# Three mask selects per head group, V left unscaled, and a back transform split by parity, in a fused attention and spectral kernel on one core

## Chip, cores and metric

The kernel runs on one core of a Trainium2 chip. The metric is the device time of one execution in microseconds, as the median of several runs. TensorE is called PE (its weight loads PEld), VectorE DVE, ScalarE ACT, GpSimd POOL and SyncE SP, as the profile does.

## What is computed

The input `x` has 2048 tokens of 640 values. Two branches read it, and a gate per token mixes them: `out = g * a + (1 - g) * b`, with `g = sigmoid(sum(x * gate_w))`.

Branch a is attention with a memory, 32 heads of 20 values, in four segments of 512 tokens:

```
for s in range(4):
    p = softmax(q_s k_s^T * scale + causal mask)
    a_dot = p @ v_s
    a_mem = (phi(q_s) @ M) / (phi(q_s) @ z + 1e-6)
    o_s = sigmoid(beta) * a_mem + (1 - sigmoid(beta)) * a_dot
    M += phi(k_s)^T @ v_s ;  z += sum of phi(k_s)
a = concat(o_s) @ wo          # phi(t) = t + 1 where t > 0, else exp(t)
```

Branch b is a filter in the frequency domain: `b = irfft2(rfft2(x) * (w_r + 1j * w_i))` over tokens and values, in float32, then rounded to bfloat16. Softmax is computed without subtracting a maximum, and its sum comes from a column of ones beside V.

## The kernel before

**Order.** The program doesn't rely on program order in Python. `record` (L934) makes a list of some 2300 operations, each with the buffers that it reads and writes and with one or two engines that could run it. The tuple `ORDER` (L708) then lists all of them: an entry halved is the operation's number, and its lowest bit picks the first or second engine of its list. `schedule` (L112) takes each engine's queue from that, gives PSUM banks and DMA semaphores by a small time model, and `emit` (L254) writes the instructions, each engine's in its queue's order, with waits on semaphores. So every engine runs in order, and an instruction that waits holds up all that is behind it on its engine. SP issues nearly all DMAs in the same way. `ENDED` (L586) is a second list, the order in which operations end; it decides only which of several waits of one instruction stands first. Operations made by `either` (L541) may stand on DVE or on POOL, those made by `copy_alts` (L526) on ACT or on DVE, and `one` (L535) names a single engine. `lock` marks DVE operations that the time model lets wait for POOL.

**Attention.** `project` (L1040) makes q, k and V of a segment; q and k go through DRAM (qk_scr) to padded tiles (qkp). `v_part` (L1229) makes V of 128 tokens for half of the heads. For odd blocks of tokens the two halves of 64 tokens change places, which the matmuls do by writing to the two halves of the PSUM bank; one DVE operation (L1244) then evicts 320 columns and multiplies them by 1 - sigmoid(beta) of each head. `attend` (L1294) handles heads in eight groups of four. Two groups make a pair with five units (`UNITS`, `qk_unit`, L1356): kinds a and b for each group and one unit of kind c for both, 80 units in all. A unit's QK matmuls fill four PSUM banks (the whole pool qk), and ACT's exp (L1393) evicts them to the tile ex, which has room for three groups. `PIECES` lists the matmuls; kind a and c use halves of the array 64 columns wide, kind b all 128. After each exp, POOL's selects (`mask`, L1411, at L1414) put zeros above the diagonal, seven per group: two after a, two after b, three after c. Then `pv_flipped` (L1307, segments 0 to 2) or `pv_group` (L1419, segment 3) multiplies by V. `denominators` (L1331) inverts the sums of a segment and sends them through DRAM (r_scr, and r back), after which `normal` (L1656) multiplies them in.

**Spectral branch.** `fft` (L1495) runs beside all this: `fold` (L1020) prepares x, F1 and D are the forward transforms over tokens and values, T twiddles, `W_mul` (L1569) multiplies by the filter, `W_add` (L1574) combines, Tb twiddles back, and Db (L1601) transforms back over values. D uses the parity of the frequency: its evicted result Bt is put in natural order by a write with a stride of two. Db doesn't: each of 16 token residues n2 and each of two types (cosine and sine) takes three matmuls of 321 columns. The cosine bank is evicted to eo in float32 (one of three buffers), and two DVE operations (L1615) add and subtract the sine bank to give the left and the mirrored right half of G.

**End.** `finish_tile` (L1636) makes the last transform over tokens, with the gate in its table (Fb), adds the projection with wo in the same PSUM bank, evicts and stores.

## Time and profile before

| | |
|---|---|
| median of 3 timed runs | 241.27 us (241.19 to 241.69) |
| span of the profiled execution, first to last instruction | 247.9 us |
| mean granted TensorE clock | 0.972 |
| busy: PE, PEld | 230.0, 139.7 us |
| busy: DVE, ACT, POOL | 196.3, 199.7, 165.7 us |
| instructions: DVE, ACT, POOL | 481, 241, 297 |

The profiled execution is one other than the timed ones. Its span is longer than their median by 6.6 us; no time of its own beside the span is given. Busy time is the union of an engine's instructions. A matmul's length holds its passage through the array, so PE counts as busy for longer than columns stream in. Short waits that end in another engine's work are listed by the releaser.

### The profile page before, as it was taken

The numbers are of one execution on the slowest core, as the hardware profiler recorded it, in microseconds if no ns is written. First come the engines' busy times: TensorE is split into PE (matmuls) and PEld (weight loads), VectorE is DVE, ScalarE is ACT, GpSimd is POOL, SyncE is SP. The second block draws the span as 40 slices with busy tenths as digits, with TensorE's granted clock in tenths as the row PEclk, the third lists the DMA queues.
The fourth block names the chain that finished last, engine by engine and source line by source line (L and its number), as shares of the span: only waits on it lengthen the run. The fifth ranks groups of instructions, "written<-read, shape, count | busy, mean of one in ns | idle before, by whom it ended". The sixth has DMA issues, their size and how long they took to land.

```text
span 247.9 us, 9233 instructions
## 1 busy us (share of the span) xinstructions
PE 230.0 (93%) x3849; PEld 139.7 (56%) x3849; DVE 196.3 (79%) x481; ACT 199.7 (81%) x241; POOL 165.7 (67%) x297
## 2 busy tenths in 40 slices
PE   7899999999999999998899999999999975699994
PEld 2574667765465665545566554455444543366794
DVE  0489998799999987888998979979888831755653
ACT  2289688998999989999999899999999864278740
POOL 8532278367969658478939998949898660559640
PEclk9999999999999999999999999999999995599999
DMA  7999979937875864768697543447665977382123
GB/s 174 281 361 206 229 191 230 269 91 203 222 173 163 199 213 114 206 95 252 170 242 208 165 131 99 122 146 192 188 183 128 282 101 81 35 118 81 59 81 109
DMA packets 58924, 42.11 MB, mean 170 GB/s; under 512 B 30020, under 2 KB 55172, under 8 KB 58884
## 3 DMA queue, kind: packets, MB, share of 16 engines
q1 hardware_dynamic: 57844, 40.96, 66.4%
q8 instruction: 30, 0.49, 0.8%
q10 hardware_dynamic: 1040, 0.57, 0.8%
q14 instruction: 10, 0.08, 0.2%
HBM read 23.32 MB, written 12.30 MB: 144 GB/s over the span
## 4 chain that ended last, share of the span: by engine, by line
PE 59%; DVE 15%; DMA 12%; ACT 8%; SPq 3%; issue 2%; DVEq 0%
PE psum L521 52%; PE psum L519 6%; ACT ex L1393 5%; DMA r<-r_scr 3%; DMA r_scr<-rc 3%; DVE Pt L1569 3%; DMA Wt<-in_B_w_i_dram 2%; DMA wk<-in_A_wk_dram 2%; DMA qk_scr<-qu 2%; SPq L553 2%; DVE G L1615 1%; SPq L555 1%; DVE oU L1656 1%; DVE phk L1213 1%; DVE va L1244 1%
## 5 line engine op out<-in xcount | busy, mean ns | idle before, releaser
L1393 ACT ACTIVATE ex<-psum 128x2048 bf16<-128x2048 f32 (+4 forms) x92 | 138.7, 1507 | 13.2 <-PE psum L521 11.4
L1414 POOL TENSOR_SCALAR_AFFINE_SELECT ex<-ex 128x256 bf16<-128x256 bf16 (+2 forms) x224 | 121.0, 562 | 41.2 <-ACT ex L1393 38.3
L521 PE MATMUL psum<-qkp 20*64 20x64 bf16 (+5 forms) x1024 | 31.8, 268 | 4.0 <-ACT ex L1393 2.1
L521 PE MATMUL psum<-xT,wk 128*128 128x256 bf16 (+1 forms) x280 | 33.9, 273 | 0.6 <-DMA wk<-in_A_wk_dram 0.6
L521 PE MATMUL psum<-xT,wq 128*128 128x512 bf16 (+1 forms) x135 | 30.7, 381 | 0.5 <-DMA xT<-in_A_x_dram 0.5
L521 PE MATMUL psum<-wv,xT 128*64 128x320 bf16 (+3 forms) x240 | 30.1, 303 | 0.3 <-DVE va L1244 0.3
L1569 DVE TENSOR_TENSOR Pt<-psum,Wt 128x642 bf16<-128x642 f32 x32 | 25.5, 821 | 2.6 <-PE psum L521 1.5
L521 PEld LDWEIGHTS psum<-qkp 20*64 20x64 bf16 (+1 forms) x1024 | 12.2, 101 | 22.0 <-ACT ex L1393 14.8
L521 PEld LDWEIGHTS psum<-xT,wk 128*128 128x128 bf16 (+1 forms) x280 | 19.9, 97 | 7.1 <-DMA wk<-in_A_wk_dram 1.6
L519 PE MATMUL psum<-wo,oU 128*32 128x320 bf16 x480 | 23.5, 317 | 0.2 <-DVE oU L1664 0.2
L1035 POOL TENSOR_TENSOR xsb<-xf 128x320 bf16<-128x320 bf16 (+2 forms) x12 | 9.5, 788 | 16.2 <-DVE xsb L1035 12.2
L1244 DVE TENSOR_TENSOR va<-psum,ebx 128x320 bf16<-128x320 f32 x32 | 15.2, 483 | 5.0 <-ACT gate L1242 2.9
L521 PEld LDWEIGHTS psum<-wv,xT 128*64 128x64 bf16 (+1 forms) x240 | 14.9, 105 | 7.4 <-issue 2.9
L532 DVE CAST ot<-psum 128x320 bf16<-128x320 f32 x21 | 10.1, 491 | 11.2 <-PE psum L519 8.8
L521 PE MATMUL psum<-big,Cp 128*128 128x321 bf16 (+1 forms) x96 | 18.7, 310 | 0.2 <-DVE G L1615 0.2
L521 PE MATMUL psum<-big,Ac 128*128 128x160 bf16 (+2 forms) x96 | 18.1, 257 | 0.3 <-DVE Pt L1569 0.2
L521 PE MATMUL psum<-ex,va 128*32 128x512 bf16 (+4 forms) x480 | 17.3, 275 | 0.5 <-DVE mem L1289 0.2
L521 PE MATMUL psum<-tt,Yt 128*128 128x256 bf16 (+1 forms) x96 | 16.5, 276 | 1.1 <-DVE Pt L1569 0.4
L1615 DVE TENSOR_TENSOR G<-eo,psum 128x320 bf16<-128x320 f32 x32 | 14.7, 482 | 3.5 <-PE psum L521 2.5
L1201 ACT ACTIVATE et<-qu 128x512 bf16<-128x512 bf16 x25 | 15.6, 629 | 0.2
L519 PEld LDWEIGHTS psum<-wo,oU 128*32 128x32 bf16 x480 | 12.5, 100 | 5.7 <-issue 1.1
L521 PEld LDWEIGHTS psum<-ex,va 128*32 128x32 bf16 x480 | 10.1, 96 | 9.8 <-POOL ex L1414 1.7
(99 smaller groups left out, 393.7 us busy)
## 6 DMA issues: line engine op xcount, KB each, us to landing
qkp<-qk_scr SPq DMA_DIRECT2D x28, 160.0 KB
tt<-tab_tt SPq DMA_DIRECT2D x8, 512.0 KB, 3.8
qk_scr<-qu SPq DMA_DIRECT2D x12, 256.0 KB, 2.4
u_scr<-ub SPq DMA_DIRECT2D x12, 256.0 KB, 4.4
xsb<-in_A_x_dram SPq DMA_DIRECT2D x8, 320.0 KB, 5.9
oU<-u_scr SPq DMA_DIRECT2D x15, 128.0 KB, 4.0
out_dram<-ot SPq DMA_DIRECT2D x12, 160.0 KB
Wt<-in_B_w_r_dram SPq DMA_DIRECT2D x16, 80.2 KB, 3.3
```

The source lines that it names most:

```text
L519: h = e.matmul(dst, wt, r_, start=st, stop=sp_, **{**kw, "tile_position": (0, q), "skip_group_check": True})
L521: h = e.matmul(o_, l_, r_, start=st, stop=sp_, **kw)
L532: alts["dve"] = (lambda e: e.tensor_copy(dst(), src()), 67 + 1.04 * n, 68.0)
L553: return e.dma_start_transpose(d_, s_)
L555: return e.dma_start(d_, s_)
L1035: self.either(lambda e, dst=dst, src=src, d0=d0, n=n, op=op: e.tensor_tensor(xs.ap(o + dst, [D, 2], [1, n]), xf.ap(src + d0, [321, 2], [1, ...
L1201: self.one("act", lambda e: e.activation(et.ap(0, [1, L]), qsl(), ACT.Exp), L, [qb], [b("et", pi_)], late, name="phi_exp")
L1244: self.one("dve", lambda e: e.tensor_tensor(va.ap(i * H * VW + h0 * VW, [VW, nh], [1, DH]), self.ps(bank, 0, [DH, nh], [1, DH]), self.ebx. ...
L1393: self.one("act", lambda e, d=d, q=q: e.activation(self.ex.ap(*d), self.ps(bank, *q), ACT.Exp, scale=SC), n, [bank], [self.exb(s, 2 * pr + ...
L1414: self.one("pool", lambda e: e.affine_select(self.ex.ap(e0 + d0, [1280, 4], [1, n], np_=np_), self.ex.ap(e0 + s0, [1280, 4], [1, n], np_=np_),
L1569: self.one("dve", lambda e, ri=ri, Pt=Pt, Wt=Wt, wo_=wo_, bank=bank: e.tensor_tensor(Pt.ap(ri * 322, [644, 2], [1, KD]), self.ps(bank, 0, ...
L1615: self.one("dve", lambda e, q=q, n2=n2, bank=bank, eo=eo: e.tensor_tensor(self.G.ap(n2 * D + 639 * q, [1 - 2 * q, 320]), eo.ap(q, [1, 320] ...
```

## The change

The change has these parts.

- **Masks.** POOL runs three selects per group in place of seven: `mask_first` (512 elements), `mask_odd` and `mask_even` (1024 each). They follow the third (kind c) unit of the pair for its first group, and the last (second b) unit for its second group. The layout of ex changes for it.
- **QK.** Kind b takes five pieces of 64 columns of the array in place of two of 128, kind c four in place of three. In segment 3 the exps of kind b and c are one operation each, where they were two.
- **V.** V isn't scaled. Odd blocks are projected as the even ones; their eviction is two copies of 64 partitions that change places, on ACT or DVE. The factor 1 - sigmoid(beta) goes into `den_gate` (segments 0 to 2) and into a table g3 (segment 3). A few small operations and one small DMA make these factors.
- **Forward side.** Bt is evicted as it lies, without a stride; W_mul reads W with a stride of two in its place, so that everything up to Db is in order of parity.
- **Back transform.** Db takes matmuls of 322, 161 and 161 columns. The cosine bank goes to eo (two buffers of 644 floats). Two DVE operations put sum and difference with the sine bank into eo, and four operations of 161 or 159 columns (`sum_G`, on DVE or POOL, both inputs in SBUF) make G from these. The table big is 2576 columns wide, not 3220.
- **Order.** `ORDER` is a new list of 2267 operations, and `ENDED` is gone: its place takes the end by the time model. The 80 units stand in the same sequence as before. By the new list sum_G stands 51 times on DVE and 13 times on POOL; V's 48 copies 18 times on ACT and 30 on DVE; folds 44 times on DVE and 4 on POOL (35 and 13 before); the evictions of Db 15 times on ACT and 1 on DVE (10 and 6), those of F1 7 and 13 (11 and 9), those of the first projections 1 and 3 (3 and 1).

```diff
-VPIECES = ((0, 0, 512, 0), (1, 512, 384, 128), (2, 896, 192, 320), (2, 1088, 64, 256), (3, 1216, 128, 384))
+VPIECES = ((0, 0, 512, 0), (1, 512, 128, 128), (1, 896, 256, 256), (2, 640, 256, 256), (3, 1152, 128, 384))
...
-              ((1, 0, 0, 192, 0, 320), (2, 0, 0, 320, 320, 192)),
-              ((2, 0, 0, 256, 0, 64), (3, 64, 64, 384, 0, 128), (3, 0, 0, 448, 64, 64)))
+              ((2, 0, 0, 256, 0, 256), (3, 64, 64, 384, 0, 64), (2, 64, 64, 320, 64, 192), (1, 0, 0, 256, 256, 256), (1, 64, 64, 256, 256, 256)),
+              ((1, 0, 0, 192, 0, 64), (1, 64, 64, 192, 0, 64), (3, 0, 0, 448, 256, 64), (3, 64, 64, 448, 256, 64)))
...
-            for p0, t0, n in ((0, 64, 64), (64, 0, 64)) if i % 2 else ((0, 0, P),):
...
-        self.one("dve", lambda e: e.tensor_tensor(
-            va.ap(i * H * VW + h0 * VW, [VW, nh], [1, DH]), self.ps(bank, 0, [DH, nh], [1, DH]),
-            self.ebx.ap(H + h0, [1, nh], [0, DH]), ALU.mult), nh * DH, [bank, b("omgh")], [vb], prio, name="ev_v")
+        for p0, p1, n in ((0, 64, 64), (64, 0, 64)) if i % 2 else ((0, 0, P),):
+            self.Sc.op(self.copy_alts(lambda p0=p0, n=n: va.ap(i * H * VW + h0 * VW, [VW, nh], [1, DH], p0=p0, np_=n),
+                                      lambda p1=p1, n=n: self.ps(bank, 0, [DH, nh], [1, DH], p0=p1, np_=n), nh * DH),
+                       r=[bank], w=[vb], prio=prio, name="ev_v")
...
+        if u == 3:
+            self.mask(s, 2 * pr, prio)
+        elif u == 4:
+            self.mask(s, 2 * pr + 1, prio)
...
+        x = [self.exb(s, g, k) for k in ("a0", "b0", "c0", "m0")]
+        self.one("pool", sel(512, 0, 64, 64, P), 512, x[:2], x[3:], prio, per=0.793, fix=218, name="mask_first")
+        self.one("pool", sel(512, 512, P, -64, 64), 1024, [], x[2:], prio, per=0.793, fix=218, name="mask_odd")
+        self.one("pool", sel(0, 0, P, 0, P), 1024, [], x[:2], prio, per=0.793, fix=218, name="mask_even")
...
-                for c in range(3):
+                for n_, (c, c0, n, tc) in enumerate(((1, 0, 322, 161), (0, 0, 161, 0), (2, 161, 161, 483))):
...
+                for q, op in enumerate((ALU.add, ALU.subtract)):
+                    self.one("dve", lambda e, q=q, op=op, bank=bank, eo=eo: e.tensor_tensor(
+                        eo.ap(322 - 322 * q, [1, 322]), eo.ap(0, [1, 322]), self.ps(bank, 0, [1, 322]), op),
+                        322, [bank, eb[0]][:2 - q], [eb[1 - q]], prio, name="sum_Db", after=[b("xT", i, c) for i in range(k + 1) for c in range(5)] if not q else ())
+                o = n2 * D
+                for d0, d1, step, n, t, op in ((0, 0, 1, 161, 322, ALU.add), (1, 319, -1, 159, 0, ALU.subtract), (0, 320, 1, 161, 322, ALU.subtract),
+                                               (1, 639, -1, 159, 0, ALU.add)):
+                    fn = lambda e, d0=d0, d1=d1, step=step, n=n, t=t, op=op, o=o, eo=eo: e.tensor_tensor(
+                        self.G.ap(o + d1, [step, n]), eo.ap(t + 161 + d0, [1, n]), eo.ap(t + d0, [1, n]), op)
+                    self.Sc.op({"dve": (fn, 67 + 1.04 * n, 68.0), "pool": (fn, 132 + 1.95 * n, 50.0)}, r=[eb[t > 0]], w=[b("G", n2, d1 // 320 if d1 != 320 else 1)],
+                               prio=prio, name="sum_G", after=acb, lock=True)
```

186 lines of the change are left out of this document (84 added, 102 removed), and 310 rows, old and new, of tables (ENDED, ORDER).

## Prediction

> **What bounds the kernel now.** I read the busy table by stretch of time first, cut where the exponential (ex, L1393) of attention unit 0, 8, 16, 56, 64 and 72 starts (of 80, counted from 0), because both orders run the 80 units in the same sequence. Columns: stretch, its length, then busy us of PE, PEld, DVE, ACT and POOL with their instruction counts, granted clock, DMA share, GB/s.
>
> ```profile
> core 0 of [0], span 247.9 us
> core 0: us, PE busy (x) PEld busy (x) DVE busy (x) ACT busy (x) POOL busy (x), PEclk, DMA share, GB/s
> 13.50:49.00 35.50, 35.16 (x438) 23.93 (x437) 32.35 (x79) 31.25 (x49) 17.79 (x31) 1.00 0.99 244
> 49.00:71.10 22.10, 21.41 (x301) 12.28 (x298) 21.20 (x58) 20.21 (x24) 15.59 (x30) 1.00 0.70 183
> 71.10:168.00 96.90, 93.30 (x1366) 53.67 (x1364) 86.68 (x206) 91.59 (x102) 74.42 (x139) 1.00 0.62 166
> 168.00:186.50 18.50, 17.48 (x275) 9.45 (x278) 16.77 (x50) 17.34 (x21) 16.72 (x30) 1.00 0.67 190
> 186.50:215.10 28.60, 22.03 (x503) 12.83 (x499) 17.78 (x45) 17.63 (x21) 15.33 (x27) 0.80 0.67 125
> 215.10:247.90 32.80, 29.59 (x828) 22.00 (x824) 17.09 (x40) 18.58 (x23) 17.02 (x31) 0.97 0.43 89
> ```
>
> The reader is to see three full engines. Up to 186.5 us PE, ACT and DVE are each busy 88 to 99% of every stretch; from 71 to 168 ACT leaves 5.3 us of 96.9 free and DVE 10.2. POOL, which the change relieves most, has the least to do in each. After 186.5 us DVE and ACT have room, and PE has the work.
>
> The chain of waits shows the one long hole, in the stretch from 186.5 (columns: start, us, what):
>
> ```profile
> 195.92 6.75 DMA r_scr<-rc
> 202.69 7.07 DMA r<-r_scr
> 209.78 1.77 DVE oU L1656 x5
> ```
>
> The third segment's reciprocal denominators go to DRAM and back in 13.8 us, and DVE, PE and ACT stand in line behind the five products that need them: PE is busy for 22.03 of 28.60 us, 6.6 us idle, at a clock of 0.80. The profiled execution spans 247.9 us, the median of the timed runs is 241.27, 6.6 us less; so part of this hole may not be there in the timed runs. I sum against the 247.9 and carry the difference over to 241.27.
>
> **The change part by part.** Engine and place of every operation were counted in the two orders, which name them by number.
>
> *Back transform (Db).* Before, three matmuls of 321 columns for each of 32 banks; after, one of 322 and two of 161. The forward transform has this shape already (columns: min/median/max ns; 321 is its longest form, 160 and 161 the short ones):
>
> ```profile
> L521 PE MATMUL psum<-big,Ac x96: 230/240/310, 49.6 to 153.8; 128*128 128x160 bf16 x32, 128*128 128x321 bf16 x32, 128*128 128x161 bf16 x32
> L521 PE MATMUL psum<-big,Cp x96: 297/301/475, 166.5 to 206.5; 128*128 128x321 bf16 x64, 65*128 65x321 bf16 x32
> ```
>
> 301 against about 236 for a short one (between the 230 and the 240) is 65 ns, twice per bank: 32 x 0.13 = 4.2 us less on PE, between 166 and 207 us. There ACT and DVE are as full as PE, and after 186.5 PE's idle time is the hole. I credit 1.0; the bounds are 0 and 4.2.
>
> *QK.* The second kind of unit goes from 8 matmuls 128 columns wide to 20 that are 64 wide; the first kind has that width now, in 12:
>
> ```profile
> 123.08 0.40 PE L521 MATMUL psum<-qkp 20*128 20x320 bf16 x8 [0.23 <-ACT ex L1393]
> ...
> 125.67 0.43 PE L521 MATMUL psum<-qkp 20*64 20x512 bf16 x12
> ```
>
> The same 512 columns stream past both halves of the array together, so 0.03 us more, x32 = 1.0 us; were each change of weights in the three-piece half to cost that again, 3 us. All four qk banks are one buffer, so exp waits for QK: I take +1.0 on the path (0 to 3).
>
> *V and its eviction.* DVE's 32 scaled evictions become 48 plain copies, 18 on ACT and 30 on DVE. In segment 3 the second exp is no longer split in two, nor the third. Db's evictions move by 5 from DVE to ACT, F1's by 4 and the first projections' by 2 the other way.
>
> ```profile
> L1393 ACT ACTIVATE ex<-psum 128x2048 bf16<-128x2048 f32 x56 | 105.2, 1879 | 7.9 <-PE psum L521 6.7
> ...
> L1393 ACT ACTIVATE ex<-psum 128x1024 bf16<-128x1024 f32 x12 | 12.3, 1023 | 1.1 <-PE psum L521 0.8
> ...
> L1393 ACT ACTIVATE ex<-psum 128x1280 bf16<-128x1280 f32 x8 | 9.9, 1239 | 3.0 <-PE psum L521 3.0
> L530 ACT ACTIVATE Ac<-psum 128x512 bf16<-128x512 f32 x11 | 6.5, 603 | 1.2 <-PE psum L521 1.2
> L1393 ACT ACTIVATE ex<-psum 128x768 bf16<-128x768 f32 x8 | 6.5, 810 | 0.3
> L530 ACT ACTIVATE Bt<-psum 128x322 bf16<-128x322 f32 x12 | 6.3, 541 | 1.5 <-PE psum L521 1.4
> ...
> L1393 ACT ACTIVATE ex<-psum 128x512 bf16<-128x512 f32 x8 | 4.8, 598 | 1.1 <-PE psum L521 1.0
> L530 ACT ACTIVATE ot<-psum 128x320 bf16<-128x320 f32 x11 | 4.7, 436 | 10.7 <-PE psum L519 8.1 <-PE psum L521 1.7 <-DMA out_dram<-ot 0.8
> L530 ACT ACTIVATE eo<-psum 128x321 f32<-128x321 f32 x10 | 4.1, 438 | 0.3 <-PE psum L521 0.3
> ```
>
> ACT: +18 x 0.436 + 5 x 0.438 = +10.0; -8 x (1.239 + 0.810 - 1.879) - 4 x (2 x 0.598 - 1.023) = -2.1; -6 x 0.603 = -3.6; Bt is written without a stride, -12 x 0.10 (541 against 438 ns) = -1.2; eight fewer one-column gate exps on top, unpriced. Net +3.1 at most. By the orders the excess lies before 49 us, where ACT has 4.3 us free; behind that its load is level. +0.5 (0 to 3.1).
>
> *DVE, early.* Nine fold operations come over from POOL, and six F1 and projection evictions from ACT:
>
> ```profile
> L1035 DVE TENSOR_TENSOR xsb<-xf x20: 310/324/844, 9.0 to 34.9; 128x320 bf16<-128x320 bf16 x8, 128x318 bf16<-128x318 bf16 x6, 128x322 bf16<-128x322 bf16 x6
> ```
>
> 9 x 0.32 = 2.9 us, and 6 at no less than ACT's 0.60 = 3.6; three V copies and four other projection evictions come after 49 us instead, 7 x 0.48 (G's 320 columns from PSUM, below) = 3.4. Net about +3 by 71 us, where DVE is busy for 53.6 of 57.6 us. What waits behind these in DVE's queue is V's eviction and phi of k, and PE behind their banks. I take +2.0 (0 to 3).
>
> *DVE, late.* Before, G came from PSUM in two operations per n2. After, two go to a float buffer, and four of about 160 columns, with both inputs in SBUF, make G: 64 in all, 51 on DVE (22 of them between 168 and 186.5 us, 22 between 186.5 and 215, 7 later), 13 on POOL.
>
> ```profile
> L1120 DVE TENSOR_TENSOR ebg<-gate,ebx x1: 257/257/257, 54.7 to 54.7; 128x128 f32<-128x128 f32 x1
> ```
> ```profile
> 186.34 1.67 DVE L1615 TENSOR_TENSOR G<-eo,psum 128x320 bf16<-128x320 f32 x4
> ```
> ```profile
> L1615 DVE TENSOR_TENSOR G<-eo,psum x32: 475/481/489, 169.2 to 217.5; 128x320 bf16<-128x320 f32 x32
> ```
> ```profile
> L1574 DVE TENSOR_TENSOR Yt<-Pt x16: 314/320/719, 56.0 to 161.7; 128x321 bf16<-128x321 bf16 x16
> ```
>
> From 257 ns at 128 columns and 481 at 320 (1.17 ns a column) 160 columns take 0.29 us. Four G operations in 1.67 us start every 0.40, 0.08 under their length, so each new one takes 0.21 of DVE's time: 51 x 0.21 = 10.7 us. And they wait: an operation with one PSUM input never strays (475 to 489), one with two SBUF inputs has the same median as minimum and a longest of 719 beside 314, with POOL running. At 0 to 0.4 us each that is 0 to 20 us; I take 0.1, 5 us. From 168 to 186.5, 22 x 0.31 = 6.8 us come to a DVE with 1.7 free; against that stand 4 fewer of the old G operations and 3 Db evictions (7 x 0.40 = 2.8), and by the counts 0.5 of smaller ones. 6.8 - 3.3 - 1.7 = 1.8; I take +1.5 (0 to 8.4, the end worked out with the rival). From 186.5 on DVE has 26 us free, and I charge nothing.
>
> By the Trainium skill, "SBUF — State Buffer", "Who interferes with whom", a DVE instruction with two SBUF inputs contends with a GpSimd instruction that reads SBUF, and whichever issues first holds the shared pair for its whole length. The spread of Yt beside that of G agrees. By this rule alone a G operation could wait out a whole select, which is the rival on DVE below.
>
> *Masks.* POOL runs seven selects per head group now, three after (one of 512, two of 1024 elements):
>
> ```profile
> L1414 POOL TENSOR_SCALAR_AFFINE_SELECT ex<-ex 128x256 bf16<-128x256 bf16 x128 | 59.5, 476 | 38.7 <-ACT ex L1393 37.4
> L1414 POOL TENSOR_SCALAR_AFFINE_SELECT ex<-ex 64x512 bf16<-64x512 bf16 x64 | 42.6, 670 | 1.8 <-ACT ex L1393 0.9
> L1414 POOL TENSOR_SCALAR_AFFINE_SELECT ex<-ex 128x512 bf16<-128x512 bf16 x32 | 22.0, 690 | 0.6
> ```
>
> Per group 4 x 0.476 + 2 x 0.670 + 0.690 = 3.9 us before; 0.84 ns an element (690 less 476 over 256) gives 0.69 + 2 x 1.12 = 2.9 after: 32 us of POOL in all. POOL waited 37.4 us for exp, so this is off the path. But three selects can run only when the group's last exp is there. At the end:
>
> ```profile
> 231.07 5.36 POOL L1414 TENSOR_SCALAR_AFFINE_SELECT ex<-ex 128x256 bf16<-128x256 bf16 x10 [1.71 <-ACT ex L1393]
> ```
> ```profile
> 233.69 2.08 ACT L1393 ACTIVATE ex<-psum 128x1280 bf16<-128x1280 f32 x2 [0.91 <-PE psum L521]
> ```
>
> The last exp ends at 235.77, the last mask at 236.43, 0.66 us later; after, 2.9. The same delay stands before the second-last unit's exp, whose buffer is freed by those products. PE has some 2 us of projections placed in between. +1.0 (0 to 4).
>
> *The hole.* In the new order the first product that needs the third segment's denominators stands two QK units later, behind 1.02 + 1.88 = 2.9 us of exp, and the read-back follows the write at once on SP. If the 13.8 us trip recurs that is -2.9; if the timed runs have no hole, 0. I take -1.0. In exchange for Bt, DVE's 32 products with W read W with a stride of two. No row shows that: 0 to the 0.10 us of ACT's strided write for each half, 6.4 us in all; I take 0, as they read PSUM at its own pace beside it. Two float buffers in place of three cost nothing as long as DVE keeps up; what if not stands in the slow rival.
>
> Sum: -1.0 + 1.0 + 0.5 + 2.0 + 1.5 + 1.0 - 1.0 = +4.0 us: 251.9 in a profiled execution like this one, **245.3** as a median.
>
> **The rivals.**
>
> *Faster: PE's relief counts in full.* PE is the fullest engine of the first table. Every us of Db's 4.2 then shortens the end, DVE's additions fit into its free time (26 us after 186.5), and the hole gains its 2.9; QK's +1.0 and the tail's +1.0 stay: -5.1, 236.2. It decides by whether DVE keeps 95% or less between 168 and 200 us. For it: DVE's share there before is 91% and lower. Against it: ACT and DVE are at their limit when Db begins. Chance 0.30.
>
> *Slower by much: DVE becomes the bound.* Each two-input G operation waits 0.4 us, and ACT, whose Db evictions need the float buffers that DVE frees, stalls with it: 22 x 0.61 = 13.4 us, less the 1.7 free and the 3.3, is +8.4; with the early 2.0 and the tail's 1.0, +11.4: 252.7. The skill's exclusive lock is this mechanism; its price here is from the longest Yt. Chance 0.17.
>
> *Nothing moves:* ACT's exps pace the kernel, the early excess fits into the 4.3 us of ACT and 3.2 of DVE, and the tail is hidden: 241 to 241.7. Chance 0.05.
>
> *The selects don't cost what I say* (runs of 64 elements might be dearer than the slope): a third dearer, and POOL is as full as before (32 x 3.9 us), the tail 1 us longer: 246.3. This lies inside the forecast.
>
> **How the numbers follow.** Forecast, +0.6 to +8 us around its +4.0 (down 3.4 where Db and the hole each count 2.7, up 4.0 where the early DVE term and the tail reach their 3 and 4): 0.48. With the rivals: faster by over 0.2% 0.30, within 0.2% 0.05 (0.2%, half a us, is about what a measurement of this kernel can tell from no change), slower 0.65. The range runs from the fast rival to the slow one, 236.0 to 253.0, and leaves out 2 in 10. The forecast's own range is 242 to 249.
>
> **What would show it.** Busy time of DVE up by 12 to 18 us, of POOL down by 25 to 35, of PE down by 2 to 5, ACT within 3: these say that the pieces are priced rightly. The stretch from unit 56 to unit 64 longer than 18.5 us with DVE over 95% says that late DVE work sets the pace; G operations spread from 0.29 to 0.7 us say that they wait for selects. If that stretch is no longer, and the end from unit 64 shorter than 61.4 us, the fast rival is right. Last mask 2 to 3 us behind the last exp: the tail. The prediction is wrong if POOL's relief moves the exps themselves, that is, if unit 56 comes earlier than 168 us: then waits for masks paced the middle, which the first table doesn't show.

## The result, and the profile after

The changed kernel takes **254.54 us** (median of 4 runs, 253.54 to 255.66), the kernel before 241.23 in the same comparison (4 runs): a ratio of 1.0536, 95% interval 1.0496 to 1.0575. The forecast was 245.3. The direction was right, the size three times too small: +13.3 us against +4.0, and outside the range.

The profile after, cut at the same exponentials (units 0, 8, 16, 56, 64 and 72 of 80, counted from 0), columns as in the prediction:

```profile
13.30:49.80 36.50, 35.88 (x453) 23.75 (x452) 34.60 (x91) 34.62 (x57) 9.69 (x12) 1.00 0.89 215
49.80:72.90 23.10, 21.97 (x347) 12.80 (x346) 22.84 (x58) 20.86 (x27) 13.69 (x20) 1.00 0.70 172
72.90:170.90 98.00, 92.52 (x1606) 55.81 (x1605) 91.98 (x223) 90.32 (x99) 63.00 (x82) 1.00 0.68 169
170.90:194.00 23.10, 17.74 (x321) 8.80 (x320) 21.94 (x60) 17.52 (x20) 13.68 (x18) 0.71 0.68 187
194.00:217.20 23.20, 20.43 (x537) 13.06 (x532) 22.55 (x62) 18.04 (x19) 12.00 (x13) 0.99 0.58 123
217.20:253.60 36.40, 31.14 (x887) 22.62 (x886) 23.91 (x59) 18.21 (x19) 14.00 (x16) 0.94 0.35 85
```

In the prediction's profile the stretch from unit 64 to 72 took 28.6 us, because of the 13.8 us trip of the reciprocals through DRAM. A second profile of the old queues (run b_ctl below: its own time is 242.44 us, its span 240.4) shows what the timed runs of the kernel before look like:

```profile
13.60:49.20 35.60, 35.26 (x438) 23.95 (x437) 32.28 (x79) 31.24 (x49) 17.76 (x31) 1.00 1.00 241
49.20:71.30 22.10, 21.41 (x300) 12.24 (x298) 21.23 (x58) 20.23 (x24) 15.63 (x30) 1.00 0.74 182
71.30:167.80 96.50, 93.22 (x1367) 53.86 (x1365) 86.82 (x206) 91.40 (x101) 74.27 (x139) 1.00 0.64 168
167.80:186.30 18.50, 17.47 (x275) 9.45 (x278) 16.76 (x50) 17.34 (x21) 16.71 (x30) 1.00 0.68 189
186.30:207.50 21.20, 20.09 (x507) 12.26 (x503) 17.31 (x44) 17.52 (x21) 14.77 (x27) 1.00 0.82 166
207.50:240.40 32.90, 28.88 (x828) 21.51 (x820) 17.55 (x41) 18.50 (x23) 17.81 (x31) 1.00 0.49 91
```

Read one table against the other: +0.9 and +1.0 us up to unit 16, +1.5 to unit 56, **+4.6 from unit 56 to 64** (+4.4 with unrounded starts, as below), +2.0 to unit 72, **+3.5 behind it**; 13.5 together, against 13.3 timed. In the two stretches from 56 to 72 DVE is busy for 44.5 of 46.3 us, where it was busy for 34.1 of 39.7. PE goes from 94% busy in the first of them to 77%. The busy times of the whole execution, of the second profile of before and of after:

```profile
PE 227.8 (95%) x3849; PEld 138.8 (58%) x3849; DVE 196.4 (82%) x481; ACT 199.4 (83%) x241; POOL 165.8 (69%) x297
```
```profile
PE 230.8 (91%) x4281; PEld 141.7 (56%) x4281; DVE 219.4 (87%) x551; ACT 201.5 (79%) x238; POOL 131.2 (52%) x168
```

POOL gave up 34.6 us and DVE took on 23.0. What the pieces of G cost on each engine (min/median/max ns), and their groups with the selects (busy us, mean ns, idle time before them):

```profile
L1491 DVE TENSOR_TENSOR G<-eo x51: 314/321/1294, 173.5 to 230.6; 128x161 bf16<-128x161 f32 x26, 128x159 bf16<-128x159 f32 x25
L1491 POOL TENSOR_TENSOR G<-eo x13: 519/538/697, 172.5 to 222.8; 128x159 bf16<-128x159 f32 x7, 128x161 bf16<-128x161 f32 x6
```
```profile
L1283 POOL TENSOR_SCALAR_AFFINE_SELECT ex<-ex 64x1024 bf16<-64x1024 bf16 (+2 forms) x96 | 92.5, 979 | 35.3 <-ACT ex L1271 31.3
L1491 DVE TENSOR_TENSOR G<-eo 128x161 bf16<-128x161 f32 (+1 forms) x51 | 20.7, 448 | 0.0
```

A piece that waits for nobody takes 0.32 us, the longest 1.29, which is 0.32 and one whole select (0.979) more. The trace shows what the long ones wait for. 32 of the 51 overlap no operation of POOL, and none of them takes more than 0.33 us. The eleven over 0.5 us all started while an operation of POOL ran (eight times a select, three times a piece of G there), and each ended 0.18 to 0.24 us after that one's end. The chain of waits runs through them at that point (start, us, what):

```profile
173.55 2.62 DVE G L1491 x7
176.17 0.60 DVE fbg L1043
...
182.05 0.24 DVE G L1491
182.29 0.67 DVE oU L1533 x2
182.96 1.91 DVE G L1491 x2
```

Of the seven pieces in 2.62 us one took 1.24 us behind a select, and the five behind it start every 0.23 us; the two in 1.91 us (0.78 and 1.29) both waited for selects.

### The profile page after: what moved, and what is told of

Its sections match the earlier page's. It is cut to its first block, busy times and chain, and to the rows that moved or that the text cites. A ratio compares the mean times of both kernels' runs of the same rounds, so it can differ in the third digit from the quotient of the medians.

```text
span 253.6 us, 10064 instructions
## 1 busy us (share of the span) xinstructions
PE 230.8 (91%) x4281; PEld 141.7 (56%) x4281; DVE 219.4 (87%) x551; ACT 201.5 (79%) x238; POOL 131.2 (52%) x168
## 4 chain that ended last, share of the span: by engine, by line
PE 54%; DVE 29%; ACT 9%; issue 4%; DMA 2%; SPq 0%; DVEq 0%
PE psum L525 49%; ACT ex L1271 8%; PE psum L523 5%; DVE G L1491 5%; DVE eo L1485 4%; DMA xT<-in_A_x_dram 2%; DVE xsb L923 2%; DVE Pt L1438 1%; DVE ub L536 1%; DVE Cp L536 1%; DVE va L536 1%; DVE oU L1533 1%; DVE phq L1105 1%; DVE xf L918 1%; DVE ot L536 1%
## 5 line engine op out<-in xcount | busy, mean ns | idle before, releaser
L1271 ACT ACTIVATE ex<-psum 128x2048 bf16<-128x2048 f32 (+1 forms) x80 | 136.5, 1706 | 16.2 <-PE psum L525 13.8
L1283 POOL TENSOR_SCALAR_AFFINE_SELECT ex<-ex 64x1024 bf16<-64x1024 bf16 (+2 forms) x96 | 92.5, 979 | 35.3 <-ACT ex L1271 31.3
L525 PE MATMUL psum<-qkp 20*64 20x64 bf16 (+4 forms) x1536 | 33.7, 259 | 4.5 <-ACT ex L1271 4.0
L525 PE MATMUL psum<-wv,xT 128*128 128x321 bf16 (+1 forms) x160 | 29.3, 300 | 0.0
L525 PEld LDWEIGHTS psum<-qkp 20*64 20x64 bf16 x1536 | 14.9, 105 | 23.6 <-ACT ex L1271 16.9
L1438 DVE TENSOR_TENSOR Pt<-psum,Wt 128x644 bf16<-128x644 f32 x32 | 26.0, 820 | 1.6 <-PE psum L525 1.2
L1491 DVE TENSOR_TENSOR G<-eo 128x161 bf16<-128x161 f32 (+1 forms) x51 | 20.7, 448 | 0.0
L525 PE MATMUL psum<-big,Cp 128*128 128x322 bf16 (+2 forms) x96 | 16.1, 284 | 3.4 <-DVE mem L1177 1.2
L525 PE MATMUL psum<-ex,va 128*32 128x256 bf16 (+2 forms) x480 | 18.4, 286 | 0.6 <-POOL ex L1283 0.6
L1443 POOL TENSOR_TENSOR Yt<-Pt 128x322 bf16<-128x322 bf16 x18 | 13.3, 749 | 9.8 <-DVE Pt L1438 7.7
L525 PE MATMUL psum<-big,Ac 128*128 128x161 bf16 (+2 forms) x96 | 16.2, 257 | 0.1
L1093 ACT ACTIVATE et<-qu 128x512 bf16<-128x512 bf16 x25 | 15.5, 625 | 0.5 <-DVE phq L1106 0.5
```

What stands on the lines that cost most here:

```text
L525: h = e.matmul(o_, l_, r_, start=st, stop=sp_, **kw)
L1093: self.one("act", lambda e: e.activation(et.ap(0, [1, L]), qsl(), ACT.Exp), L, [qb], [b("et", pi_)], late, name="phi_exp")
L1271: self.one("act", lambda e: e.activation(self.ex.ap(*d), self.ps(bank, *q), ACT.Exp, scale=SC), n, [bank], [self.exb(s, 2 * pr + gp, ks) f ...
L1283: return lambda e: e.affine_select(self.ex.ap(e0 + d0, [640, 8], [1, n], np_=np_), self.ex.ap(e0 + s0, [640, 8], [1, n], np_=np_), [[0, 8] ...
L1438: self.one("dve", lambda e, ri=ri, Pt=Pt, Wt=Wt, wo_=wo_, bank=bank: e.tensor_tensor(Pt.ap(ri * 322, [644, 2], [161, 2], [1, 161]), self.p ...
L1443: fn = lambda e, r=r, a0=a0, a1=a1, op=op, Pt=Pt, Yt=Yt: e.tensor_tensor(Yt.ap(r * 322, [1, 322]), Pt.ap(a0 * 322, [1, 322]), Pt.ap(a1 * 3 ...
```

## The experiments

Three theories stood at the start, a fourth came on the way. T1: the pieces of G on DVE, and the port that they share with POOL's selects. T2: late masks. T3: the new order by itself. T4: PE's clock. Kernels whose name begins with a_ are made from the changed kernel, those with b_ from the one before. Where a part of one kernel was put into the other, all remaining operations kept their queues, and new ones were put where their inputs end by the planned times. The table gives the ratio to the kernel before (95% interval) and, from the trace of each, the us between the starts of exponentials 0, 16, 56, 64, 79 and the end.

| run | ratio | 0–16 | 16–56 | 56–64 | 64–79 | 79–end |
|---|---|---|---|---|---|---|
| b_ctl | 1.003 (0.998–1.008) | 57.7 | 96.5 | 18.6 | 39.8 | 14.3 |
| after | 1.0536 (1.050–1.058) | 59.6 | 98.0 | 23.0 | 42.0 | 17.7 |
| a_noS | 1.038 (1.031–1.045) | 59.6 | 98.0 | 18.8 | 43.1 | 17.3 |
| a_Gsmall | 1.030 (1.020–1.040) | 59.6 | 98.0 | 20.2 | 39.8 | 17.6 |
| a_selsmall | 1.019 (1.010–1.028) | 57.9 | 97.2 | 21.0 | 38.4 | 17.1 |
| a_noS_sel | 1.025 (1.018–1.033) | 58.0 | 97.8 | 18.8 | 41.4 | 17.6 |
| a_sellock | 1.039 (1.032–1.046) | 58.4 | 98.4 | 20.4 | 42.5 | 17.4 |
| a_sellock2 | 1.040 (1.031–1.050) | 57.9 | 98.2 | 22.0 | 41.3 | 17.8 |
| a_fill | 1.049 (1.042–1.056) | 60.0 | 98.7 | 23.1 | 41.4 | 16.9 |
| a_eo3 | 1.050 (1.041–1.059) | 60.1 | 98.5 | 23.3 | 41.4 | 17.3 |
| a_tail | 1.061 (1.049–1.072) | 60.4 | 98.0 | 23.0 | 43.6 | 18.7 |
| a_Gpool | 1.074 (1.067–1.081) | 59.7 | 98.2 | 25.4 | 45.8 | 17.3 |
| a_noV | 1.075 (1.070–1.081) | 61.3 | 103.1 | 23.4 | 42.0 | 16.2 |
| a_noM | 1.133 (1.123–1.142) | 64.0 | 102.4 | 27.7 | 47.5 | 17.2 |
| b_F | 0.997 (0.994–1.000) | 58.0 | 95.7 | 18.6 | 38.1 | 14.3 |
| b_selsmall | 0.995 (0.991–0.999) | 58.4 | 95.3 | 18.6 | 39.1 | 14.2 |
| b_V | 1.047 (1.038–1.055) | 62.5 | 100.2 | 18.8 | 41.3 | 15.2 |
| b_S3 | 1.084 (1.079–1.088) | 58.4 | 95.7 | 31.9 | 46.9 | 14.2 |
| b_M | 1.131 (1.122–1.140) | 64.1 | 106.9 | 22.8 | 48.0 | 18.2 |

### The split out of the changed kernel, and its pieces cut short

a_noS takes the forward side and the back transform of before into the changed kernel (the 64 entries of sum_G leave the order). a_Gsmall is:

```diff
-                        self.G.ap(o + d1, [step, n]), eo.ap(t + 161 + d0, [1, n]), eo.ap(t + d0, [1, n]), op)
+                        self.G.ap(o + d1, [step, 8]), eo.ap(t + 161 + d0, [1, 8]), eo.ap(t + d0, [1, 8]), op)
...
-                            self.G.ap((4 * a + q) * D + 320 * hf, [1, 320]), True, False,
+                            self.G.ap((4 * a + q) * D + 320 * hf, [0, 40], [1, 8]), True, False,
```

> The changed kernel with its three selects and unscaled V, but with the forward side and the back transform of before (Bt written with a stride, Db in three matmuls of 321 columns, G made from PSUM in two operations per n2, three float buffers of 322), in the new order without the 64 sum_G operations. Theory T1 (the pieces of G on DVE are the loss: 51 x 0.448 us, and what stands behind them): DVE's busy time falls by some 20 us from 219, the stretch from the 57th to the 72nd exponential is 6 us or more shorter, and the time is 242 to 246 us. Theory T2 (late masks: three selects of 0.98 us that can start only after the last exponential of their group): the time stays at 251 to 255 us. Theory T3 (the new order by itself, whatever the operations): 250 to 255 us, with DVE less busy and PE idle instead.

> The changed kernel with each of the 64 sum_G operations cut to 8 of its 161 or 159 columns; the rest of G isn't made, and the last transform reads the same 8 columns over and over, in as many matmuls of the same size. All waits and the order stay. T1: DVE loses 51 x some 0.3 us = 15 us or more, the time falls by 7 to 11 us to 244 to 248 us. T2: the time stays within 2 us of 254.5. T3: it stays within 3 us.

Both miss T1's time: the medians are 252.8 and 250.6 us, or 250.4 and 248.4 by the ratios. DVE's busy time fell by 15.5 and 11.5 us, less than T1 said, and in a_noS the stretch from the 57th to the 72nd exponential got only 2.5 us shorter, not 6; by its median alone a_noS fits T2 and T3. T1's place is right for the first part of that stretch. Units 56 to 64, cut out of the trace of a_noS, with the next row (64 to 72):

```profile
170.80:189.60 18.80, 15.01 (x321) 7.81 (x321) 14.45 (x38) 17.18 (x19) 7.63 (x9) 1.00 0.64 179
189.60:215.70 26.10, 24.04 (x541) 14.37 (x536) 18.54 (x42) 17.97 (x20) 11.26 (x12) 0.87 0.75 146
```

18.8 us, against 23.0 with the split and 18.6 before: in this stretch the split is the whole loss, and DVE's load is its form (14.45 us in place of 21.94). But a part of the gain is given back at once: the next row takes 26.1 us, 2.9 more than in the changed kernel. There the chain has two DMAs, one behind the other in SP's queue:

```profile
189.57 6.29 DMA u_scr<-ub
...
197.88 5.16 DMA gbc<-g_scr
```

So the whole split, with its stalls, is worth 1.5% here, and the columns of the pieces alone 2.4% (the two intervals overlap). With the short pieces the units 64 to 79 take 39.8 us, as in b_ctl. Pieces of 8 columns still take 0.15 us each, and the longest waits nearly as long (0.92 us over the shortest, where it was 0.98):

```profile
L1491 DVE TENSOR_TENSOR G<-eo x51: 148/158/1065, 173.0 to 225.3; 128x8 bf16<-128x8 f32 x51
```

### The split alone in the old order

The forward side and the split, with three float buffers, in the kernel before; sum_G stands behind its second sum.

> The kernel before with the forward side and the split back transform of the change alone, with three float buffers, the sum_G operations right behind their second sum (51 on DVE and 13 on POOL as in the change); seven selects, scaled V and the other queues as before. T1: DVE's busy time rises by some 18 to 25 us from 196, and the time by 4 to 8 us to 245 to 250. If the split is worth something to PE, it rises by 2 or less.

+8.4%, some 20 us, beyond every theory. The row of units 56 to 64 and the pieces of G:

```profile
166.90:197.90 31.00, 22.14 (x264) 11.64 (x265) 29.05 (x76) 17.95 (x21) 21.56 (x38) 0.61 0.45 125
```
```profile
L1509 DVE TENSOR_TENSOR G<-eo x51: 266/501/1914, 169.0 to 227.5; 128x161 bf16<-128x161 f32 x26, 128x159 bf16<-128x159 f32 x25
```

Up to unit 56 and in the tail it is as fast as b_ctl (58.4, 95.7, 14.2 us); all of the loss lies where Db is. The median piece takes 0.50 us here, 0.32 in the changed kernel, as 29 of the 51 take more than 0.4 us and not 11. The number of selects alone doesn't do this: a_noM (below), with seven per group in the new order, has a median of 0.32 and 19 such pieces. How often a piece meets a select depends on the order, too.

### The selects cut short

In a_selsmall two of the three selects handle 64 elements in place of 1024; b_selsmall cuts the five that work in place in the kernel before to as many (`[1, 16]` in four runs).

```diff
-            return lambda e: e.affine_select(self.ex.ap(e0 + d0, [640, 8], [1, n], np_=np_), self.ex.ap(e0 + s0, [640, 8], [1, n], np_=np_),
-                                             [[0, 8], [1, n]], ALU.is_ge, 0.0, base=base, channel_multiplier=-1)
+            return lambda e: e.affine_select(self.ex.ap(e0 + d0, [640, 8], [1, 64 if d0 != s0 else 8], np_=np_), self.ex.ap(e0 + s0, [640, 8], [1, 64 if d0 != s0 else 8], np_=np_),
+                                             [[0, 8], [1, 64 if d0 != s0 else 8]], ALU.is_ge, 0.0, base=base, channel_multiplier=-1)
```

The expectation of b_selsmall names two ratios: they are those of a_noS and a_selsmall.

> The changed kernel with two of its three selects (1024 elements) cut to 64 elements; so most of the upper triangle is not set to zero. POOL loses some 55 us or more of busy time. T1 with the lock: G operations fall from a mean of 0.448 to 0.33 us with a maximum below 0.7, folds and Yt become shorter too, the gain of 3 to 6 us arises between the 57th and the 72nd exponential, and the tail (from the last exponential to the end) gives at most 2 us. T2: the tail shortens by 2 us or more and the middle units come earlier; G operations keep their length. Both give a time of 248 to 252 us; the place of the gain and the length of the G operations tell them apart.

> The kernel before with five of its seven selects per group (those in place) cut to 64 elements, so that most of the upper triangle is not set to zero: the control for the same cut in the changed kernel, which gave 1.0381 - 1.019 and more. If POOL's selects slow DVE's two-input operations by the lock in any kernel, DVE's busy time falls by 3 to 8 us here too (196 before) and the time by 1 to 4 us. If the price is that of late masks, which this kernel doesn't have, the time stays within 1 us.

The largest gain of all in the changed kernel, 1.0536 to 1.019 (8.4 us by the ratios), and 0.5% in the kernel before, where DVE's busy time falls by 3.1 us (196.4 to 193.3). In a_selsmall DVE's falls by 9.2, and half of that is G:

```profile
L1491 DVE TENSOR_TENSOR G<-eo x51: 306/319/799, 170.7 to 221.7; 128x161 bf16<-128x161 f32 x26, 128x159 bf16<-128x159 f32 x25
```

The same medians, but a longest of 0.80, where T1 said less than 0.7. The tail hardly shortens (17.1), which speaks against T2 at that place; the gain lies in 0–16, 56–64 and 64–79. The cut takes away load and lateness at once. These two put the load back, on memory that nobody else reads:

```diff
...
+        for _ in range(3):
+            self.one("pool", lambda e: e.affine_select(self.idle.ap(0, [1, 352]), self.idle.ap(0, [1, 352]), [[1, 352]], ...), 352, [], [self.b("idle")], ...)
```

> The changed kernel with two of its three selects cut to 64 elements, as in a_selsmall, and behind the last of each group three selects of 352 elements on memory of their own that no other instruction reads (32 x 3 x some 0.5 us = 48 us of POOL, about what the cut took away, 52). Nothing on the path waits for them but the next group's selects. If POOL's load on the shared port was the price, G operations go back from a mean of 0.358 to 0.42 us or more, DVE's busy time from 210 to 215 or more, and the time from 247.8 to 251 to 255 us. If the lateness of the masks was the price, the time stays at 246 to 250 us.

> As a_sellock (two of three selects cut to 64 elements; 96 selects of 352 elements on memory that no other instruction reads, 47 us of POOL), but the added selects stand in POOL's queue only where it had a gap of at least their length before its next mask. If POOL's load on the shared port is the price, the time is 250.5 to 254 us again and DVE's busy time 214 us or more. If lateness is the price, the time is 247 to 249 us, DVE's busy time may still be 214.

Both came to 252 us: of the 8.4, some 5 come back with the load. DVE's busy time is 215.0 and 214.7 (210.2 without), a piece of G takes 0.40 us on average (0.36 without, 0.45 in the changed kernel). In a_sellock2 the masks don't get late again. What follows the last exponential there, which ends at 235.13 us:

```profile
235.19 1.25 POOL L1290 TENSOR_SCALAR_AFFINE_SELECT ex<-ex 128x512 bf16<-128x512 bf16 x3 [1.87 <-ACT ex L1278]
237.29 0.79 POOL L1339 TENSOR_TENSOR on<-on,mem 128x320 bf16<-128x320 bf16 x1 [0.84 <-DVE on L1334]
238.03 1.66 POOL L1297 TENSOR_SCALAR_AFFINE_SELECT idle<-idle 128x352 bf16<-128x352 bf16 x3
```

The last mask ends 1.3 us behind that exponential, as in a_selsmall (2.9 in the changed kernel). Measured in every group against the same exponential (the one after which its first mask can run), the last mask ends 5.2 us later on average, 5.1 in a_selsmall and 6.4 in the changed kernel. So POOL's load by itself is the larger part of the 8.4 us. The remaining 3 go with late masks or with the load that isn't back (POOL is busy for 124.7 us, not 131.2); these two aren't told apart. By place the load counts in 64–79 (38.4 us without it, 42.5 and 41.3 with it). In 0–16 it doesn't: 57.9 us in a_sellock2 with POOL busy there for 22.4 us (23.4 in the changed kernel).

### All pieces on POOL, and three float buffers

a_Gpool sets the lowest bit of all 64 entries of sum_G in the order. a_eo3 is:

```diff
...
-        self.eo = [T(f"eo{i}", [P, 644], F32, at=self.xT[0].off + i * 2592) for i in range(2)]
+        self.eo = [T(f"eo{i}", [P, 644], F32, at=self.xT[0].off + i * 2592) for i in range(3)]
...
-                k = n2 % 2
+                k = n2 % 3
...
```

> The changed kernel with all 64 sum_G operations on POOL, none on DVE; otherwise the same order. T1: DVE's busy time falls by 18 us or more, POOL's rises by 51 x 0.54 = 28 us; selects and G operations stand in one queue, so the masks come later; the time falls by 2 to 6 us if DVE's load was the price. T2 (late masks): it rises by 2 us or more.

> The changed kernel with three float buffers eo of 644 columns in place of two (the broadcast reciprocals of the third segment move to other memory). If ACT's evictions of Db, which waited 3.9 us for DVE's G operations, stall the exponentials and PE, the time falls by 1.5 to 4 us. If DVE's own queue is what counts, the time stays within 1 us of 254.5.

On POOL a piece takes 0.53 us (median of 64), and the ratio is 1.074, 4.9 us slower than the change, as T2 had it. T1's own number missed: DVE lost the 20.7 us of its pieces, and its busy time fell by 2.5 us only (219.4 to 216.9). Other operations with two inputs in SBUF took the time, as they now wait for POOL's pieces. Two of them, first in the changed kernel, then in a_Gpool:

```profile
L1043 DVE TENSOR_TENSOR fbg<-fcat,gbc x4: 670/682/814, 176.1 to 233.5; 128x512 bf16<-128x512 bf16 x4
L1541 DVE TENSOR_TENSOR oU<-oU,mT x8: 481/484/1449, 201.3 to 236.7; 128x640 bf16<-128x640 bf16 x8
```
```profile
L1043 DVE TENSOR_TENSOR fbg<-fcat,gbc x4: 679/844/5157, 171.6 to 238.0; 128x512 bf16<-128x512 bf16 x4
L1541 DVE TENSOR_TENSOR oU<-oU,mT x8: 481/756/4643, 199.8 to 241.0; 128x640 bf16<-128x640 bf16 x8
```

The operation of 5.16 us met a select on POOL, seven pieces and one more select ran there one behind the other, and it ended 0.55 us after the last of them: it didn't get in between. So moving work to POOL didn't free DVE. Three buffers gain nothing that can be seen (1.050, the intervals lie on one another): the stall of ACT behind the two float buffers, a part of the slow rival, had no price that these runs resolve.

### PE's clock

In the changed kernel the clock is halved for the time in which the most is lost. Four stretches of its trace; the seventh number is the granted clock:

```profile
173.80:177.20 3.40, 2.17 (x62) 1.23 (x54) 3.40 (x9) 2.65 (x4) 1.02 (x1) 1.00 0.92 128
177.20:180.60 3.40, 1.88 (x43) 1.00 (x44) 3.37 (x10) 3.15 (x4) 1.80 (x4) 1.00 0.85 279
180.60:194.30 13.70, 11.59 (x168) 5.25 (x168) 12.28 (x35) 9.17 (x10) 8.33 (x10) 0.50 0.59 179
194.30:197.70 3.40, 2.68 (x51) 1.45 (x49) 3.23 (x8) 3.00 (x3) 1.16 (x2) 1.00 0.41 118
```

Is this cause or consequence? a_fill gives PE more to do just there:

```diff
-                    self.mms([(th, n)], cpb + [b("big"), bank], [], prio, name="Db", mode=0)
+                    self.mms([(th, n)] * (3 if n_ == 0 and 1 <= n2 <= 5 else 1), cpb + [b("big"), bank], [], prio, name="Db", mode=0, ...)
```

> The changed kernel with more to do for PE and nothing else: in the ten banks of Db of n2 = 1 to 5, which stand between 170 and 188 us, the first matmul (322 columns) is issued three times, each overwriting the one before; the result is the same. A third theory, T4 (PE's clock): in the profiled run of the changed kernel PE was busy for only 56% of the 3.4 us before 180.64 us, and from there on the granted clock was 0.50 for 13.65 us. T4: with 2.7 us more of matmuls in this place PE stays above some two thirds, the clock stays at 1.00, PE's busy time falls from 230.8 to some 228 in spite of the added work, the stretch from the 61st to the 65th exponential takes 10 to 11 us in place of 13.3, and the time falls by 3 to 6 us to 249 to 252. T1 (DVE alone sets the pace there, 97% busy): the clock may rise, but the time stays within 1.5 us of 254.5, or rises.

```profile
173.80:177.20 3.40, 2.81 (x69) 1.69 (x62) 3.36 (x11) 2.54 (x5) 0.68 (x2) 1.00 0.98 114
177.20:182.50 5.30, 3.92 (x88) 2.14 (x80) 5.23 (x16) 4.99 (x7) 3.03 (x4) 1.00 0.75 212
182.50:185.90 3.40, 1.41 (x41) 0.88 (x41) 3.40 (x10) 2.27 (x3) 2.34 (x3) 1.00 0.32 90
185.90:192.80 6.90, 6.44 (x76) 2.56 (x76) 6.15 (x19) 3.62 (x4) 3.48 (x6) 0.51 0.80 251
```

The clock stayed whole for 7 us longer (180.6 and 185.9 us; the first exponential was at 13.3 and 11.2), the halved stretch shrank from 13.7 to 6.9 us, and units 56 to 64 took 23.1 us, no less than without (23.0). DVE is the busy column in the first three rows (3.36 of 3.40, 5.23 of 5.30, 3.40 of 3.40). T4 falls, as a price of 3 to 6 us: DVE sets the pace, PE starves, and the halved clock follows.

### The tail

The last QK, the work behind it and the last store, cut at the last exponential's start and at PE's end: b_ctl, after, and a_tail, which moves twelve of PE's operations ahead of the last QK.

```profile
226.10:237.20 11.10, 11.02 (x316) 9.73 (x315) 6.64 (x17) 4.50 (x7) 4.30 (x8) 1.00 0.26 78
237.20:240.40 3.20, 0.00 (x0) 0.00 (x0) 0.47 (x1) 0.00 (x0) 0.00 (x0) 1.00 0.45 127
```
```profile
235.90:249.00 13.10, 13.05 (x384) 11.27 (x379) 8.19 (x22) 5.03 (x7) 4.24 (x5) 1.00 0.27 83
249.00:253.60 4.60, 0.00 (x0) 0.00 (x0) 0.49 (x1) 0.00 (x0) 0.00 (x0) 0.86 0.30 83
```

PE is never idle up to its end; it has 384 matmuls behind the last exponential's start, not 316, and takes 2.0 us longer. From PE's end to the end it is 4.6 us in place of 3.2. This goes with one part of the change: in the 13 profiles of kernels with unscaled V, whose SP issues 233 DMAs and not 232, it is 3.8 to 4.8 us, in the 7 with scaled V 3.2 to 3.3. The traces place the difference: near PE's end one issue of a store on SP, on ACT or on both takes 0.9 to 2.2 us in the former, and in the latter none takes more than 1.0, some 2.5 us earlier. Why is open. Of the 68 more matmuls 40 are products of the exponentials with V, which now come behind later masks, and 28 belong to Fb and to products with wo. The products with V in the same stretch, of b_ctl and of after:

```profile
L519 PE MATMUL psum<-va,ex 128*128 128x21 bf16 x80 | 2.5, 172 | 0.0
```
```profile
L525 PE MATMUL psum<-va,ex 128*128 128x21 bf16 x120 | 3.3, 172 | 0.0
```

> The changed kernel with twelve operations of PE (two Fb and ten products with wo, for the last tile of the second segment), their two evictions and the sum before them moved ahead of the last QK; the old order has six of these twelve there. If the longer tail is PE's work that the new order leaves behind the last unit, the stretch from the 80th exponential to the end falls from 17.7 to some 15.5 us, the 80th exponential comes later by less than that, and the time falls by 0 to 1.5 us. If the tail hangs on the late masks, it stays at 17 us or more.

```profile
236.40:250.60 14.20, 12.95 (x336) 10.54 (x328) 7.10 (x21) 5.01 (x7) 3.58 (x4) 0.88 0.22 65
```

With 48 matmuls fewer the tail is longer, not shorter (the whole run, 1.061, isn't told apart from the change), and the units ahead of it come later (43.6 us from 64 to 79): PE now idles for 1.2 us, most of it (0.9) until DVE has evicted an ot, and its clock is halved for 3.4 us. So this move of the products of an earlier tile gained nothing; that part of my reading isn't borne out. That it was the late masks for which PE waited isn't shown either: no wait of PE in this tail ends in a select.

### Masks and V by themselves, in either order

b_M and b_V put one part into the kernel before, a_noM and a_noV take one out of the changed kernel.

> The kernel before with the masks of the change alone: three selects per group, the QK pieces of 64 columns, one exponential per unit in segment 3; each engine's queue otherwise as before, the selects standing where their last exponential ends. T1: within 2 us of before, 240 to 243.5 us, as POOL's relief is worth nothing and the tail costs 1 to 2. T2: 245 us or more. T3: within 1 us of before.

> The changed kernel with the masks of before: seven selects per group, each behind its own exponential, QK in 64- and 128-column pieces, segment 3's exponentials in 96 parts altogether as before; unscaled V and the split back transform stay, and each engine's queue otherwise too. T2 (late masks hold up the products with V): the time falls by 5 us or more against the changed kernel (254.5), to 249 or less, and the tail from the last exponential to the end is 2 to 3 us shorter. T1 with the lock (POOL's selects lengthen DVE's two-input operations): POOL has some 32 us more to do, DVE's busy time rises by 1 to 4 us, and the time rises by 0 to 4 us.

> The kernel before with unscaled V alone: 48 plain copies (18 on ACT, 30 on DVE, as in the change) in the places of the 32 scaled evictions, the factor in the later operations. T1: DVE's load is about level, ACT's rises by 8 us; the time is 0 to 3 us above before. T2 and T3: within 1 us of before.

> The changed kernel with V scaled at its eviction as before: 32 operations on DVE in place of 48 copies on DVE and ACT, odd blocks projected to two halves, the factors small as before. The three other parts and the new order stay. If unscaled V has a share in the loss, the time falls by 1.5 to 5 us from 254.5. If the loss lies in the pieces of G, the selects and the order, it stays within 1.5 us.

All four are slower than the kernel that they are made from, by 2 to 13%, in both directions of the same edit, and slower than expected. So they don't price a part: they show that an order made for one set of operations is bad for the other, with the added ones placed by planned times. The three additions to the old order cost 13.1, 4.7 and 8.4%, 26 if they add up; the change with its own order costs 5.4, so the new order seems to save much of what the parts cost in the old one. That doesn't decide T3: no run has the operations of before alone in the new order.

### Both causes away, and controls

> Both together: the changed kernel with the back transform and forward side of before, and with two of the three selects cut to 64 elements. If the pieces of G and POOL's selects (their time on a shared port or their lateness) are all of the loss, the time is within 2 us of before, 240 to 244. If the new order or the rest of the change has a price of its own, it stays at 246 us or more.

> The kernel before with the same queues on each engine, its list sorted by planned start, and the waits of one instruction ordered by planned end in place of the list ENDED: a control for the kernels made from the old order, and a second profile. If the hole of 195.9 to 209.8 us (r_scr to DRAM and back) belongs to that one profiled execution, the span is 238 to 242 us now and the 72nd to 73rd exponential are 2 to 4 us apart, not 8.9; if it belongs to the kernel, it stands there again. The time is within 0.5% of before either way.

> The kernel before with the forward side of the change alone: Bt evicted without a stride, W read with a stride of two, everything up to Db in order of parity, and Db's three matmuls of 321 columns with their table's rows in that order; no split, no pieces of G. Evictions of Bt get 0.03 (DVE) to 0.10 us (ACT) shorter, the 32 products with W stay at 0.82 us. The time falls by 0.3 to 1.5 us if these evictions pace the middle, and stays within 0.3 us if not.

a_noS_sel is a_noS with the short selects. b_ctl sorts the old list by planned start and drops ENDED. b_F takes Bt, W_mul and the order of parity from the change and keeps Db's three matmuls, with the rows of their table permuted:

```diff
+        q[:160], q[161:322] = t[1:321:2], t[0:321:2]
```

a_noS_sel stays 2.5% above before, no better than a_selsmall by itself: the two causes overlap, and some 6 us remain that neither explains. They lie in the tail (+3.3, of which 1.3 stand behind PE's end), in 64–79 (+1.6) and in 16–56 (+1.3). PE's clock has no part in them, as it is whole in this trace up to the last stores. What of this is unscaled V, narrower QK pieces or the order (T3) is open. b_ctl has no hole:

```profile
198.38 4.14 DMA r<-r_scr
202.53 0.02 issue
202.55 1.77 DVE oU L1532 x5
```

4.1 us for the read-back, PE fed meanwhile, 2.9 us from unit 71 to 72 where the first profile had 8.9. b_F, the forward side alone, measures 0.997 (0.994 to 1.000): a gain of some 0.3%, at most 0.6, at the limit of what is resolved, and of the parts put into the old order the only one that cost nothing.

## Why the prediction was wrong

Against b_ctl, step by step:

- **DVE, late: the step that failed.** Priced +1.5 up to unit 64 and nothing behind it ("From 186.5 on DVE has 26 us free, and I charge nothing"). Measured: +4.4 from 56 to 64, nearly all of which goes with the split (18.8 us in a_noS, 18.6 before), and +2.2 from 64 to 79, which is gone with pieces of 8 columns (a_Gsmall). The mechanism was named, and its sizes were off. The 51 pieces fill 20.7 us of DVE's time, not 51 x (0.21 + 0.1) = 15.8: without a wait they start every 0.23 us, which is near the 0.21, and the wait beside POOL was priced too low (0.17 by these numbers, not 0.1). In 56–64 the 22 pieces fill 9.3 us, priced were 6.8, and of the 1.7 us that were counted as free 1.2 stayed idle. Behind unit 64 the price was nothing. The 26 us free there were a sum over two stretches: 10.8 stood in the stretch with the hole of one profiled execution, and the rest comes after unit 72. In b_ctl DVE has 3.9 us free from 64 to 72, where 22 pieces fill 8.4 us; in the change 0.7 are left.
- **The slow rival** had the mechanism (two-input operations on the shared port, DVE as the bound) and, with 252.7, the time nearest to the measured. That its time came so near is luck. It had 8.4 us up to unit 64 where 4.4 were measured, a wait of 0.4 us for each piece where the mean is 0.13 over the median, nothing behind unit 64, and 1.0 for the tail, which measured 3.4. Its other half, ACT behind two float buffers, was worth nothing that showed (a_eo3). It got 0.17 where the row for it, Yt's longest of 719 beside a median of 320, was already there.
- **The tail.** +1.0 (0 to 4) against +3.4. The last mask is 2.9 us behind the last exponential as said. But PE has 2.0 us more to do behind that exponential, 40 products with V among it, and the end comes 1.4 us later behind PE's, which no step had and which the profiles show with unscaled V only. Why the units ahead don't come earlier by that work is open.
- **The hole.** -1.0 was credited for a gain that the timed runs can't have: the hole belonged to one profiled execution (from 64 to 72 b_ctl, b_F and b_selsmall take 20.6 to 21.2 us, not 28.6). The prediction named that possibility and still summed against that span. The 0 for W read with a stride was right: W_mul's median is 820 ns in b_ctl and 822 in the change.
- **DVE, early:** +2.0 against +1.9, but by another cause than the folds: with short selects the stretch is 57.9 us, as before, with the folds unchanged, and it stays so with POOL's load put back (a_sellock2). So the number was right by luck; late masks are what is left as the cause, which isn't shown.
- **QK, and ACT:** +1.0 and +0.5 against +1.5 from 16 to 56, not told apart. **Db on PE:** -1.0 isn't seen, though the matmuls got as short as priced (the median of the 96 is 244 ns, 301 before). PE's busy time is 227.0 us in a_selsmall against 227.8, with 13.7 us of it at half the clock, so the two kernels can't be compared by it.
- Of the signs named: POOL -34.6 (25 to 35) and ACT +2.1 (within 3) were right; DVE +23.0 (12 to 18) and PE +3.0 (-2 to -5; the halved clock is in it) were not. Units 56 to 64 longer than 18.5 us with DVE at 95%, and pieces spread from 0.31 to 1.29 us, came as the signs for late DVE work and for waits behind selects.

## What to carry to other kernels

Where two engines share a port, price an operation moved onto the fuller of them by its mean beside the other's load, not by its best case, and in each stretch against the time that is free there. Before free time is counted on, take a second profile: here 7 us of DVE's 26 were an accident of the first. And where queues are ordered by hand, a part taken alone into the old order measures the order, too: the same split cost 8.4% there and 1.5% (taken out) in an order made for it.

## What the hardware showed

- PE's clock was halved without PE being idle. 1.88 of 3.40 us busy (55%) were followed by 13.65 us at 0.50; over all profiles, the 3.4 us ahead of each halving inside the kernels have PE busy for 12 to 88%, most of them 41 to 72. The halved stretches last 3.41 us or a multiple of it (3.41, 6.83, 10.24, 13.65, up to 30.72). By the Trainium skill, "TensorE: Matmul & The Clock Gate", "What's actually happening", half rate comes after an idle window of some 3.4 us and full rate after a busy one; the length of the steps agrees, the idle window doesn't: here a half-busy one was enough.
- An operation of DVE that meets one of POOL on the shared port waits for its end: the eleven long pieces of G ended 0.18 to 0.24 us after it. With work queued on POOL it waits for several in a row (5.16 us, a_Gpool).
- DVE operations with one SBUF input wait for POOL, too. The first operation of phi of q, in the changed kernel and with short selects (x15 each):

```profile
L1105 DVE TENSOR_SCALAR phq<-qu x15: 230/283/1182, 34.4 to 162.9; 128x512 bf16<-128x512 bf16 x15
```
```profile
L1105 DVE TENSOR_SCALAR phq<-qu x15: 228/283/824, 34.1 to 161.0; 128x512 bf16<-128x512 bf16 x15
```

  By the Trainium skill, "SBUF — State Buffer", "Who interferes with whom", tensor_scalar in a two-port mode takes the shared pair and contends with GpSimd as a two-input tensor_tensor does; the longest of 1182 agrees, as it ended 0.15 us after a select that it met. Not all of these waits are for selects: the 824 with short selects, and two of 826 and 814 in the changed kernel, ended as long after a Yt on POOL. I had looked for two-input operations only.
